# Attention and gated MLP on one core: the first batch in two halves of its queries, its projections woven into the same batch

## The chip, the cores and the metric

The kernel runs on 1 core of one Trainium2 chip. The metric is the device time of one execution in microseconds (us). The engines are PE (TensorE: matmuls and transposes), PEld (its weight loads), ACT (ScalarE), DVE (VectorE), POOL (GpSimd) and SP (SyncE, which here only starts DMAs); PSUM is the memory that the matmuls write.

## The reference, cut to what matters

```
q, k, v: (8 batches, 8 heads, 576 tokens, 64)
scores = q k^T / 8;  keep scores >= rowmax - tau;  softmax of those;  attn = softmax v
x  = attn, as (4608 tokens, 512)
h  = x w_in            (512 -> 2048)
g  = h * clip(h + 3, 0, 6) / 6
out = g w_out          (2048 -> 512)
```

## The kernel before

Two heads make a pair, two pairs a "quad", and a quad is worked off in nine slots: four blocks of 128 queries for each pair, and one slot for the 64 rest queries of both. The program is a loop of 144 slots, 18 to a batch, and a tail. In each slot the engines do this:

```python
for n, sl in enumerate(queue):
    ...
    exp(previous slot) x2                     # ACT
    sm_max(sl)                                # DVE: copy scores out of PSUM, row maximum; POOL: bias = tau - max
    if slot != 8 and todo1:                   # one projection step: 8 matmuls with w_in, relu, gate
        i, j = todo1.pop(0); ...
    sm_recip(prev)                            # DVE: the reciprocal, once per slot
    ... mm2_part(...)                         # quarters of an output tile: 4 matmuls with w_out
    mask(sl) x2                               # ACT
    ... transposes of q and k, or an av product (attn = p v), each evicted from PSUM
    queue[n + 1].tiles = scores(...)          # PE: the next slot's scores
    sm_norm(prev)                             # POOL: normalise x2; SP: DMA transpose of p, for the av product
    start(loads, 2 if n < 3 else 1)           # q and k, by SP
    start(vcasts, 1 if n else 0)              # v, cast to bf16, issued by POOL
    if n > 6:
        start(casts, 1)                       # w_in then w_out, cast to bf16, issued by POOL
```

Each engine works in the program's order here: what stands waits for its own data, and what is behind it waits too. Batch 0's projections are handed over at slot 22, when all its heads and queries are done. The scores take PSUM from a pool of two tiles, av and the q/k transposes share one PSUM tile.

## Time and profile before

| | |
|---|---|
| time | 592.41 us median of 3 |
| span of the profiled execution | 589.8 us |
| busy: PE, ACT, DVE, POOL | 94%, 81%, 70%, 52% |
| first reciprocal, that of slot 18, of slot 63 | 15.56, 72.10, 232.00 us |

The reciprocal occurs once a slot, so its start times are a clock of the slots ("slot n" below is the stretch from the n-th reciprocal to the next). The lines of the profile that carry the argument stand in the prediction. To them I add the first batch in one stretch (stretch, its length, busy us and count on PE, PEld, DVE, ACT, POOL, then granted clock of PE, DMA share, GB/s), and the waits in it (engine and line, what it waited for, total us, times, longest).

```profile
15.56:72.10 56.54, 44.59 (x241) 24.18 (x240) 29.24 (x90) 52.35 (x123) 42.78 (x87) 0.84 1.12 174
```

```profile
ACT s L218 <- POOL bias L213: 3.9, 4, 1.8
```

```profile
PE tp L152 <- ACT qT L156: 4.2, 3, 1.9
PE s L189 <- DVE s L210: 2.3, 3, 0.9
PE av L245 <- ACT kT L174: 2.2, 2, 2.0
```

ACT is busy 52.35 of 56.54 us (the fourth busy figure).

### The profile page before, as it was taken

How to read it: one execution, taken by the hardware profiler on the slowest of the kernel's cores; microseconds unless marked ns; L12 is line 12 of the kernel's file. 1: busy time of each engine (PE TensorE's matmuls, PEld its weight loads, DVE VectorE, ACT ScalarE, POOL GpSimd, SP SyncE). 2: the span in 40 equal slices, each digit the busy share in tenths (PEclk: the TensorE clock that was granted, in tenths of full speed). 3: DMA queues.
4: the chain of work that ended last, by engine and by line, in shares of the span. 5: the costliest groups of instructions: out<-in, count | busy, mean ns of one | idle time of the engine just before them, and what ended most of it. 6: DMA issues, size and time to landing. Idle time of an engine off the chain costs nothing. (4 is left out here: it accounts for less than half of the span.)

```text
span 589.8 us, 11554 instructions
## 1 busy us (share of the span) xinstructions
PE 552.3 (94%) x3840; PEld 319.8 (54%) x3840; DVE 412.4 (70%) x1008; ACT 480.0 (81%) x1078; POOL 305.5 (52%) x646
## 2 busy tenths in 40 slices
PE   6887698889999999999999999999999999999997
PEld 3544354545556555656556565655556565554663
DVE  1545467777878887888868787888868787872350
ACT  4999899798889898898878988898879989881340
POOL 0769676875555555654555555654555555550000
PEclk9978689989999999999999999999999999999999
DMA  5999999999697768976697758985698746552101
GB/s 116 142 178 191 180 152 192 163 177 154 132 154 150 154 119 152 152 155 137 140 137 155 151 119 163 141 162 126 133 138 158 153 101 108 97 110 69 54 19 71
DMA packets 269498, 80.45 MB, mean 136 GB/s; under 512 B 252544, under 2 KB 264832, under 8 KB 269440
## 3 DMA queue, kind: packets, MB, share of 16 engines
q1 hardware_dynamic: 252032, 70.81, 63.4%
q0 software_dynamic: 17408, 8.92, 13.5%
q8 instruction: 30, 0.49, 0.4%
q14 instruction: 28, 0.23, 0.1%
HBM read 36.70 MB, written 9.44 MB: 78 GB/s over the span
## 5 line engine op out<-in xcount | busy, mean ns | idle before, releaser
L230 POOL TENSOR_SCALAR pn<-s,rinv 128x576 bf16<-128x576 f32 x288 | 211.6, 745 | 143.8 <-issue 89.3
L210 DVE TENSOR_SCALAR_CACHE_REDUCE s<-s 128x576 f32<-128x576 f32 x288 | 206.7, 755 | 86.6 <-PE s L189 69.1
L218 ACT ACTIVATE s<-s,bias 128x576 f32<-128x576 f32 x288 | 207.3, 767 | 56.1 <-POOL bias L213 55.3
L222 ACT ACTIVATE s<-s 128x576 f32<-128x576 f32 x288 | 192.9, 672 | 0.4
L189 PE MATMUL s<-kT,qT 64*128 64x288 f32 x1024 | 178.2, 450 | 3.4 <-DVE s L210 2.3
L274 PE MATMUL h<-xT,w_in_sb 128*128 128x288 bf16 x1024 | 144.6, 287 | 3.5 <-DVE g L290 2.8
L302 PE MATMUL o<-w_out_sb,g 128*128 128x512 bf16 x576 | 139.9, 379 | 3.9 <-DVE osb L310 3.9
L274 PEld LDWEIGHTS <-w_in_sb 128*128 128x128 bf16 x1024 | 91.6, 98 | 65.8 <-issue 21.1
L189 PEld LDWEIGHTS s<-kT,qT 64*128 64x128 f32 x1024 | 98.6, 195 | 49.7 <-DVE s L210 12.8
L290 DVE SCALAR_TENSOR_TENSOR g<-r,h 128x576 bf16<-128x576 f32 x128 | 96.5, 754 | 26.1 <-ACT r L282 23.3
L213 POOL TENSOR_SCALAR bias<-m 128x1 f32<-128x1 f32 x288 | 54.6, 190 | 79.0 <-DVE s L210 58.3
L302 PEld LDWEIGHTS <-g 128*128 128x128 bf16 x576 | 55.6, 98 | 59.6 <-issue 9.9
L284 DVE TENSOR_SCALAR r<-h 128x576 f32<-128x576 f32 x81 | 61.0, 753 | 0.0
L222 ACT ACTIVATION_READ_ACCUMULATOR s<-s 128x1 f32 x288 | 54.4, 189 | 0.0
L282 ACT ACTIVATE r<-h,three 128x576 f32<-128x576 f32 x47 | 34.5, 736 | 12.3 <-PE h L274 11.8
L245 PE MATMUL av<-pT,vm 128*64 128x512 bf16 x256 | 36.0, 405 | 8.0 <-ACT kT L174 6.3
L310 DVE TENSOR_SCALAR osb<-o 128x512 f32<-128x512 f32 x30 | 20.3, 678 | 29.3 <-PE o L302 28.6
L245 PEld LDWEIGHTS <-vm 128*64 128x64 bf16 x512 | 20.3, 112 | 33.5 <-issue 26.8
L225 DVE RECIPROCAL rinv<-rsum 128x2 f32<-128x2 f32 x144 | 23.0, 160 | 21.2 <-ACT s L222 20.8
L308 ACT ACTIVATE osb<-o 128x512 f32<-128x512 f32 x6 | 3.6, 597 | 30.4 <-PE o L302 30.4
L152 PE MATMUL tp<-identf,km 128*128 128x128 f32 x128 | 20.9, 288 | 7.1 <-ACT qT L156 7.1
L258 DVE CAST xT<-av 128x512 bf16<-128x512 f32 x32 | 21.8, 682 | 6.3 <-PE av L249 6.3
(32 smaller groups left out, 270.5 us busy)
## 6 DMA issues: line engine op xcount, KB each, us to landing
qm<-in_q_dram SPq DMA_DIRECT2D x64, 128.0 KB, 3.1
km<-in_k_dram SPq DMA_DIRECT2D x64, 128.0 KB, 3.0
out_dram<-osb SPq DMA_DIRECT2D x32, 256.0 KB, 2.6
vm<-in_v_dram POOLq DMA_DIRECT2D x16, 256.0 KB, 5.9
pT<-pn SPq DMA_TRANSPOSE x128, 3.5
w_in_sb<-in_moe_w_in_dram POOLq DMA_DIRECT2D x16, 128.0 KB, 4.1
w_out_sb<-in_moe_w_out_dram POOLq DMA_DIRECT2D x16, 128.0 KB, 3.6
qr<-in_q_dram SPq DMA_DIRECT2D x16, 64.0 KB, 2.7
```

The lines of the kernel that those rows point to most:

```text
L189: nc.tensor.matmul(tiles[a][:, hf, 0:HALF], qkT[pair][0][a * 64:(a + 1) * 64, t * P:(t + 1) * P], keys(pair, a, hf), start=True, stop=True)
L210: nc.vector.tensor_scalar(out=sl.s[:, i, :].rearrange("p (a b) -> p a b", a=2), in0=ps[:, :, 0:HALF], scalar1=1.0, scalar2=None, op0=Alu.m ...
L213: nc.gpsimd.tensor_scalar(out=sl.bias[:, i:i + 1], in0=sl.m[:, i:i + 1], scalar1=-1.0, scalar2=tau, op0=Alu.mult, op1=Alu.add)
L218: nc.scalar.activation(out=s, in_=s, func=Act.Prelu, bias=sl.bias[:, i:i + 1], alpha=REJECT)
L222: nc.scalar.activation(out=s, in_=s, func=Act.Exp, accum_out=sl.rsum[:, i:i + 1])
L230: nc.gpsimd.tensor_scalar(out=pn[:, i, :], in0=sl.s[:, i, :], scalar1=sl.rinv[:, i:i + 1], scalar2=1.0, op0=Alu.mult, op1=Alu.mult)
L245: nc.tensor.matmul(ps[a * 64:(a + 1) * 64, :], vm[:, 2 * hp + a, c * D:(c + 1) * D], pT[:, 5 * a + c, cols], start=(c == 0), stop=False)
L274: nc.tensor.matmul(hps[:, hf, 0:HALF], w_in_sb[:, ki, ni * P:(ni + 1) * P], xT[b][:, ki, hf * HALF:(hf + 1) * HALF], start=(ki == 0), stop ...
L282: nc.scalar.activation(out=r[:], in_=hps[:, :, 0:HALF], func=Act.Relu, bias=three[:])
L284: nc.vector.tensor_scalar(out=r[:], in0=hps[:, :, 0:HALF], scalar1=3.0, scalar2=0.0, op0=Alu.add, op1=Alu.max)
L290: nc.vector.scalar_tensor_tensor(out=g.rearrange("p (a b) -> p a b", a=2), in0=r[:], scalar=6.0, in1=hps[:, :, 0:HALF], op0=Alu.min, op1=A ...
L302: nc.tensor.matmul(o_ps[0], gbuf[:, ni, mt * P:(mt + 1) * P], w_out_sb[:, ni, :], start=(ni == 0), stop=(ni == NI - 1))
```

## The change

The intent: while the first batch runs, PE has nothing to project, and later it is the bound. So batch 0's queries are taken in two halves over all heads. After the first half (256 tokens) its projections can start, eleven slots earlier (the first step in slot 12 instead of 23). This needs q and k of all four pairs early, and the weights early.

```diff
-    qk_pool = ctx.enter_context(tc.tile_pool(name="qk", bufs=4))
+    qk_pool = ctx.enter_context(tc.tile_pool(name="qk", bufs=6))
...
+    for i in range(2):
+        transpose_main(1, i)()          # pair 1, ahead of the first scores
...
+    for half in range(2):
+        for pair in range(NPAIR):
+            for t in (2 * half, 2 * half + 1):
+                slot(pair, t, lambda pair=pair, t=t: first_dst(pair, t))
+            job(8 * half + 2 * pair + 5, lambda pair=pair, half=half: av_main(
+                pair, pts[(pair // 2, half)], (pair % 2) * 256, 256 * half, 256))
+    for quad in range(2):
+        slot(2 * quad, 4, lambda quad=quad: rest_dst(quad))
+        job(20 + quad, lambda quad=quad: av_rest(quad))
+    job(11, lambda: todo1.extend(moe_part(0, 0, 256, (0, 1))))
+    job(21, lambda: todo1.extend(moe_part(0, 256, 320, (2, 3))))
+    job(0, lambda: (alloc_qk(2), alloc_qk(3)) and transpose_main(2, 0))
...
-        if n > 6:
-            start(casts, 1)
+        if n > 2:
+            start(casts, 2)
```

(Cut: the bookkeeping that turns fixed slots into a list of jobs, the projection step with parts of 256 or 320 tokens, and the earlier start of the q and k loads of pairs 2 and 3. From batch 1 on all jobs stand in the same slots as before.)

More of the change, by code (lines that the diff above doesn't have):

```diff
@@ L180, in keys, with scores @@
         return kT[a * 64:(a + 1) * 64, c0:c0 + HALF]
-    def scores(quad, slot):
+    def scores(sl):
         tiles = [ps_s.tile([P, 2, 512], F32, tag="s", name="s") for _ in range(2)]
         for hf in range(2):
-            if slot < 8:
-                pair, t = 2 * quad + slot // 4, slot % 4
+            if sl.t < 4:
+                pair, t = sl.pair, sl.t
                 for a in range(2):
@@ L193, in scores @@
                     for a in range(2):
-                        pair = 2 * quad + n
+                        pair = sl.pair + n
                         nc.tensor.matmul(tiles[a][n * 64:(n + 1) * 64, hf, 0:HALF],
@@ L198, in scores @@
         return tiles
-    class Slot:
-        pass
     def sm_max(sl):
@@ L231, in sm_norm @@
                                     op0=Alu.mult, op1=Alu.mult)
-        if sl.slot < 8:
-            pair, t = 2 * sl.quad + sl.slot // 4, sl.slot % 4
-            dst = pts[pair][:, :, t * P:(t + 1) * P]
-        else:
-            dst = ptr[sl.quad][:, :, :]
+        dst = sl.dst()
         nc.sync.dma_start_transpose(out=dst, in_=pn[:].rearrange("p a b -> p (a b)"))
@@ L249, in av, with av_main @@
             nc.tensor.matmul(ps[r, :], vr[r, hp, :], pT[r, 4, cols], start=False, stop=True)
-    def av_main(pair):
+    def av_main(pair, pT, c0, o0, n):
         b, hp = divmod(pair, NPAIR)
-        if hp == 0:
+        if hp == 0 and b not in xT:
             xT[b] = x_pool.tile([P, KI, S], BF16, tag="xT", name="xT")
         ps = ps_m.tile([P, 512], F32, tag="m", name="av")
-        av(ps[:], pair, pts[pair], slice(0, 512))
-        o0 = 64 if b % 2 else 0
-        nc.vector.tensor_copy(out=xT[b][:, hp, o0:o0 + 512], in_=ps[:])
+        av(ps[:, 0:n], pair, pT, slice(c0, c0 + n))
+        o0 += 64 if b % 2 else 0
+        nc.vector.tensor_copy(out=xT[b][:, hp, o0:o0 + n], in_=ps[:, 0:n])
     def av_rest(quad):
@@ L267, in av_rest, with mm1, mm1_gate @@
                               in_=ps[:, 0:P].rearrange("p (a b) -> p a b", a=2))
-    def mm1(b, ni, pool=None):
+    def mm1(item, pool=None):
+        b, parts, w = item
         hps = (pool or ps_h).tile([P, 2, 512], F32, tag="s" if pool else "h", name="h")
-        for hf in range(2):
+        for n, (ni, c0) in enumerate(parts):
             for ki in range(KI):
-                nc.tensor.matmul(hps[:, hf, 0:HALF], w_in_sb[:, ki, ni * P:(ni + 1) * P],
-                                 xT[b][:, ki, hf * HALF:(hf + 1) * HALF], start=(ki == 0), stop=(ki == KI - 1))
-        return hps
+                nc.tensor.matmul(hps[:, n, 0:w], w_in_sb[:, ki, ni * P:(ni + 1) * P],
+                                 xT[b][:, ki, c0:c0 + w], start=(ki == 0), stop=(ki == KI - 1))
+        return hps[:, :, 0:w]
     def mm1_relu(hps, on_act):
-        r = r_pool.tile([P, 2, HALF], F32, tag="r", name="r")
+        w = hps.shape[2]
+        r = r_pool.tile([P, 2, 320], F32, tag="r", name="r")[:, :, 0:w]
         if on_act:
-            nc.scalar.activation(out=r[:], in_=hps[:, :, 0:HALF], func=Act.Relu, bias=three[:])
+            nc.scalar.activation(out=r, in_=hps, func=Act.Relu, bias=three[:])
         else:
-            nc.vector.tensor_scalar(out=r[:], in0=hps[:, :, 0:HALF], scalar1=3.0, scalar2=0.0, op0=Alu.add,
-                                    op1=Alu.max)
-        return r
-    def mm1_gate(b, ni, hps, r):
-        g = gbuf[:, ni, (b % 2) * S:(b % 2 + 1) * S]
-        nc.vector.scalar_tensor_tensor(out=g.rearrange("p (a b) -> p a b", a=2), in0=r[:], scalar=6.0,
-                                       in1=hps[:, :, 0:HALF], op0=Alu.min, op1=Alu.mult)
+            nc.vector.tensor_scalar(out=r, in0=hps, scalar1=3.0, scalar2=0.0, op0=Alu.add, op1=Alu.max)
+        return r
+    def mm1_gate(item, hps, r):
+        b, parts, w = item
+        o0 = (b % 2) * S
+        (n0, c0), (n1, c1) = parts
+        if n0 == n1:
+            g = gbuf[:, n0, o0:o0 + S].rearrange("p (a b) -> p a b", a=2)
+        else:
+            g = gbuf[:, n0:n0 + 2, o0 + c0:o0 + c0 + w]
+        nc.vector.scalar_tensor_tensor(out=g, in0=r, scalar=6.0, in1=hps, op0=Alu.min, op1=Alu.mult)
     o_ps = {}
@@ L324, in flush, with quarters, moe_part @@
         late.clear()
+    def quarters(bb, mts):
+        return [(bb, mt, part) for mt in mts for part in range(4)]
     def moe_of(b):
-        one = [(b, ni) for ni in range(NI)]
-        two = [(b // 2, mt, part) for mt in (range(4) if b % 2 == 0 else range(4, 9)) for part in range(4)]
-        return one, two
+        one = [((b, ((ni, 0), (ni, HALF)), HALF), ()) for ni in range(NI)]
+        one[-1] = (one[-1][0], quarters(b // 2, range(4) if b % 2 == 0 else range(4, 9)))
+        return one
+    def moe_part(b, c0, w, mts):
+        one = [((b, ((ni, c0), (ni + 1, c0)), w), ()) for ni in range(0, NI, 2)]
+        one[-1] = (one[-1][0], quarters(b // 2, mts))
+        return one
     alloc_qk(0)
@@ L335, with slot, job @@
     transpose_rest((0, 1))()
+    for i in range(2):
+        transpose_main(1, i)()
+    class Slot:
+        pass
     queue = []
-    for quad in range(NQUAD):
-        for slot in range(NSLOT):
-            sl = Slot()
-            sl.quad, sl.slot = quad, slot
-            queue.append(sl)
-    queue[0].tiles = scores(0, 0)
+    jobs = {}
+    def slot(pair, t, dst):
+        sl = Slot()
+        sl.pair, sl.t, sl.dst = pair, t, dst
+        queue.append(sl)
+    def job(n, f):
+        jobs.setdefault(n, []).append(f)
@@ new lines, in new_pT, with rest_dst, first_dst @@
+    def new_pT():
+        return pt_pool.tile([P, 9, 512], BF16, tag="pT", name="pT")
+    def rest_dst(quad):
+        ptr[quad] = ptr_pool.tile([P, 9, P], BF16, tag="pR", name="pR")
+        return ptr[quad][:, :, :]
+    def first_dst(pair, t):
+        key = (pair // 2, t // 2)
+        if pair % 2 == 0 and t % 2 == 0:
+            pts[key] = new_pT()
+        c0 = (pair % 2) * 256 + (t % 2) * P
+        return pts[key][:, :, c0:c0 + P]
+    for half in range(2):
[4 more added lines that the diff above has]
+                pair, pts[(pair // 2, half)], (pair % 2) * 256, 256 * half, 256))
@@ new lines @@
+    for quad in range(2):
[4 more added lines that the diff above has]
+    job(0, lambda: (alloc_qk(2), alloc_qk(3)) and transpose_main(2, 0))
+    job(1, lambda: transpose_main(2, 1))
+    job(2, lambda: transpose_rest((2, 3)))
+    job(3, lambda: transpose_main(3, 0))
+    job(4, lambda: transpose_main(3, 1))
@@ new lines, with main_dst @@
+    job(12, lambda: (alloc_qk(4), alloc_qk(5)) and transpose_main(4, 0))
+    job(14, lambda: transpose_main(4, 1))
+    job(16, lambda: transpose_rest((4, 5)))
+    def main_dst(pair, t):
+        if t == 0:
+            pts[pair] = new_pT()
+        return pts[pair][:, :, t * P:(t + 1) * P]
+    for quad in range(2, NQUAD):
+        p0 = 2 * quad
+        for pair in (p0, p0 + 1):
+            for t in range(4):
+                slot(pair, t, lambda pair=pair, t=t: main_dst(pair, t))
+        slot(p0, 4, lambda quad=quad: rest_dst(quad))
+        n0 = NSLOT * quad
+        job(n0 + 1, lambda p0=p0: transpose_main(p0 + 1, 0))
+        job(n0 + 2, lambda p0=p0: transpose_main(p0 + 1, 1))
+        if quad + 1 < NQUAD:
+            job(n0 + 5, lambda p0=p0: (alloc_qk(p0 + 2), alloc_qk(p0 + 3)) and transpose_main(p0 + 2, 0))
+            job(n0 + 6, lambda p0=p0: transpose_main(p0 + 2, 1))
+            job(n0 + 7, lambda p0=p0: transpose_rest((p0 + 2, p0 + 3)))
+        job(n0 + 8, lambda p0=p0: av_main(p0, pts[p0], 0, 0, 512))
+        job(n0 + 12, lambda p0=p0: av_main(p0 + 1, pts[p0 + 1], 0, 0, 512))
+        job(n0 + 13, lambda quad=quad: av_rest(quad))
+        if quad % 2:
+            job(n0 + 13, lambda quad=quad: todo1.extend(moe_of(quad // 2)))
@@ L345 @@
+    queue[0].tiles = scores(queue[0])
     prev = None
     for n, sl in enumerate(queue):
-        quad, slot = sl.quad, sl.slot
-        b, g = divmod(quad, 2)
-        if slot in (0, 4):
-            pts[2 * quad + slot // 4] = pt_pool.tile([P, 9, 512], BF16, tag="pT", name="pT")
-        if slot == 8:
-            ptr[quad] = ptr_pool.tile([P, 9, P], BF16, tag="pR", name="pR")
-        if quad == 0 and slot == 0:
+        quad, slot_n = divmod(n, NSLOT)
+        if n == 0:
             load_quad(1)
-        if slot == 4 and quad + 2 < NQUAD:
+            start(loads, 5)
+        if slot_n == 4 and quad + 2 < NQUAD:
@@ L356 @@
             load_quad(quad + 2)
-        if slot == 0 and g == 1 and b + 1 < B:
-            load_v(b + 1)
+        if slot_n == 0 and quad % 2 and quad // 2 + 1 < B:
+            load_v(quad // 2 + 1)
         if prev is not None:
@@ L362 @@
         sm_max(sl)
-        if slot != 8 and todo1:
-            i, j = todo1.pop(0)
-            h = mm1(i, j)
-            r = mm1_relu(h, on_act=(slot in (0, 3)))
-            mm1_gate(i, j, h, r)
-            if j == NI - 1:
-                todo2.extend(moe_of(i)[1])
+        if (slot_n != 8 or quad < 2) and todo1:
+            item, then = todo1.pop(0)
+            h = mm1(item)
+            mm1_gate(item, h, mm1_relu(h, on_act=(slot_n in (0, 3))))
+            todo2.extend(then)
         if prev is not None:
@@ L373 @@
         outs = []
-        for _ in range((2, 1, 1, 0, 1, 1, 1, 1, 1)[slot]):
+        for _ in range((2, 1, 1, 0, 1, 1, 1, 1, 1)[slot_n]):
             if todo2:
@@ L381 @@
             sm_mask(sl, i)
-        evict = None
-        nxt = 2 * quad + 2
-        if slot in (1, 2):
-            evict = transpose_main(2 * quad + 1, slot - 1)
-        elif slot == 3 and quad > 0:
-            av_main(2 * quad - 1)
-        elif slot == 4 and quad > 0:
-            av_rest(quad - 1)
-            if quad % 2 == 0:
-                todo1.extend(moe_of(quad // 2 - 1)[0])
-        elif slot in (5, 6, 7) and quad + 1 < NQUAD:
-            if slot == 5:
-                alloc_qk(nxt)
-                alloc_qk(nxt + 1)
-            evict = transpose_main(nxt, slot - 5) if slot < 7 else transpose_rest((nxt, nxt + 1))
-        elif slot == 8:
-            av_main(2 * quad)
-        if evict:
-            evict()
+        for f in jobs.get(n, ()):
+            evict = f()
+            if evict:
+                evict()
         if n + 1 < len(queue):
-            queue[n + 1].tiles = scores(queue[n + 1].quad, queue[n + 1].slot)
+            queue[n + 1].tiles = scores(queue[n + 1])
         if prev is not None:
@@ L406 @@
         late.extend(outs)
-        start(loads, 2 if n < 3 else 1)
+        start(loads, 1)
         start(vcasts, 1 if n else 0)
-        if n > 6:
-            start(casts, 1)
+        if n > 2:
+            start(casts, 2)
         prev = sl
@@ L416, with rest1, rest2, rest @@
     sm_norm(prev)
-    last = NQUAD - 1
-    steps = 0
-    def rest1(i, j):
-        nonlocal steps
-        h = mm1(i, j, pool=ps_s if steps % 3 else None)
-        steps += 1
-        mm1_gate(i, j, h, mm1_relu(h, on_act=True))
-    outs2 = 0
-    def rest2(items):
-        nonlocal outs2
-        for bb, mt, part in items:
-            mm2_part(bb, mt, part, pool=ps_s if outs2 % 3 else None)
+    count = [0, 0]
+    def rest1(item, then):
+        h = mm1(item, pool=ps_s if count[0] % 3 else None)
+        count[0] += 1
+        mm1_gate(item, h, mm1_relu(h, on_act=True))
+        todo2.extend(then)
+    def rest2():
+        while todo2:
+            bb, mt, part = todo2.pop(0)
+            mm2_part(bb, mt, part, pool=ps_s if count[1] % 3 else None)
             if part == 3:
                 flush()
-                late.extend(mm2_out(bb, mt, on_act=(outs2 % 2 == 0)))
-                outs2 += 1
-    while todo1:
-        i, j = todo1.pop(0)
-        rest1(i, j)
-        if j == NI - 1:
-            todo2.extend(moe_of(i)[1])
-    av_main(2 * last + 1)
-    rest2(todo2)
-    av_rest(last)
-    one, two = moe_of(B - 1)
-    for i, j in one:
-        rest1(i, j)
-    rest2(two)
+                late.extend(mm2_out(bb, mt, on_act=(count[1] % 2 == 0)))
+                count[1] += 1
+    def rest():
+        while todo1:
+            rest1(*todo1.pop(0))
+    n0 = NSLOT * NQUAD
+    rest()
+    jobs[n0 + 3][0]()
+    rest2()
+    for f in jobs[n0 + 4]:
+        f()
+    rest()
+    rest2()
     flush()
```

## The prediction

> **What bounds the kernel now.** I read the page first, then the busy time of each engine in stretches, then the times of single instructions. The program is a loop of 144 slots (16 groups of four heads, nine slots each; a batch is 18 slots), then a tail. VectorE does one small reciprocal per slot, so the timeline of these gives the slot clock: the first is at 15.56 us, the one of slot 9 at 41.01, 18 at 72.10, 27 at 102.71, 36 at 135.87, 45 at 167.32, 54 at 199.94; from there a group takes 32.1 to 34.2 us, mostly 32.6. I asked for the busy time between these marks (stretch, its length, busy us and count on PE, PEld, DVE, ACT, POOL, then granted clock, DMA share, GB/s):
>
> ```profile
> 0.00:15.56 15.56, 9.66 (x32) 6.06 (x32) 3.04 (x10) 6.88 (x16) 1.27 (x9) 1.00 0.48 110
> 15.56:41.01 25.45, 21.47 (x102) 11.75 (x100) 13.36 (x42) 24.68 (x59) 18.67 (x38) 0.87 1.07 168
> 41.01:72.10 31.09, 23.12 (x140) 12.43 (x140) 15.88 (x49) 27.67 (x65) 24.11 (x49) 0.83 1.17 180
> 72.10:102.71 30.61, 27.40 (x180) 16.29 (x179) 20.29 (x58) 28.87 (x67) 21.51 (x46) 0.90 1.08 173
> 102.71:135.87 33.16, 27.74 (x204) 16.85 (x203) 24.97 (x63) 28.61 (x67) 24.10 (x49) 0.95 1.11 170
> 135.87:167.32 31.45, 30.23 (x226) 17.68 (x224) 25.67 (x64) 28.83 (x67) 18.21 (x39) 1.00 0.80 138
> 167.32:199.94 32.62, 32.62 (x242) 18.95 (x240) 26.36 (x65) 28.95 (x67) 19.31 (x40) 1.00 0.90 155
> ```
>
> The reader is to see two regimes. From 167 us PE is busy the whole group, so PE sets the time. In the first four groups PE has 3 to 8 us idle per group and a granted clock of 0.83 to 0.95: ACT (97% busy in the first group) and at times POOL set the time. The PE-full group is only 1 to 2 us longer than the groups without projections: there is little to win by taking PE work away.
>
> The second view is the POOL timeline in the second group, where loads of v and casting weight loads are issued by POOL:
>
> ```profile
> 42.88 0.80 POOL L103 DMA_DIRECT2D vm<-in_v_dram  x1
> 43.68 0.54 POOL L117 DMA_DIRECT2D w_in_sb<-in_moe_w_in_dram  x1
> 44.30 0.46 POOL L213 TENSOR_SCALAR bias<-m 128x1 f32<-128x1 f32 x2
> 44.85 1.47 POOL L230 TENSOR_SCALAR pn<-s,rinv 128x576 bf16<-128x576 f32 x2
> 46.26 0.80 POOL L103 DMA_DIRECT2D vm<-in_v_dram  x1
> ```
>
> One slot of POOL here is 46.26 - 42.88 = 3.38 us: bias pair, normalise pair, v issue, one weight issue. The page doesn't count issues as busy, yet POOL does nothing else meanwhile, and the next bias stands behind them. ACT, whose own slot is two exponentials (0.67 each) and two masks (1.34), 2.68 us, then waits:
>
> ```profile
> 44.51 1.44 ACT L218 ACTIVATE s<-s,bias 128x576 f32<-128x576 f32 x2 [1.00 <-POOL bias L213]
> ```
>
> **What the Trainium skill says.** "DMA: Bandwidth & Descriptors", section "SWDGE vs HWDGE vs iDMA": a DMA that casts can only be issued by GpSimd, whose own cores write the descriptors; the trace agrees, with 0.54 to 0.60 us of POOL per weight load and 0.65 to 0.93 per v load. "TensorE: Matmul & The Clock Gate", section "What's actually happening": a PE with idle windows of about 3.4 us falls to half its clock; the 0.83 and 0.87 of the first two groups agree, and 1.00 in the full ones. "Perfetto Trace Analysis", section "Optimization Strategy": where the most contended engine changes over time, interleaving the regimes can help. That is this change's intent.
>
> **The change, part by part.** A projection step is one slot's w_in product (8 matmuls); a quarter is a fourth of an output tile (4 matmuls).
>
> Does the tail shrink? No. I listed the order of the work queue: batch 1 and all later batches are handed over at the same slots as before (batch 1 at slot 40, the last ones at slot 130 and after the loop), one step per slot. What moves is batch 0 alone: its 16 steps from slots 23 to 40 to slots 12 to 19 and 22 to 29, its 16 quarters from slots 40 to 54 to 20 to 36. So 54 slots and the start change, the rest should be as before.
>
> Start. Two more transpose rounds precede the first scores. A round is 6.31 - 4.54 = 1.77 us (PE about 1.1, ACT 0.6). The last eviction before them ends at 9.91; then 1.77 + 1.10 puts the scores at about 12.8 instead of 9.4 (when their second pair of weights was loaded): +3.4. Slot 0 now also has an eviction, 0.5 on ACT. Together **+3.9 us**. (The loads of heads 2 and 3 are issued by 7.5 us and take about 3: in time.)
>
> Slots 1 to 17. POOL without issues is 3.38 - 0.80 - 0.54 = 2.04, say 2.09 with gaps. Weight loads go from one per slot (slots 7 to 38) to two (slots 3 to 18): POOL 2.09 + 2 x 0.58 = 3.25 us, above ACT's 2.68 and above its 3.16 with a 0.48 eviction; with v 3.9 to 4.05. The larger of POOL and ACT by slot: slots 1 and 2 (ACT 3.16, 3.77) 6.9; slots 3 and 4 with v 7.8; slots 5 to 8 13.0; slots 9 to 12 with v 15.9; slots 13 to 17 16.75 (slot 16 has six small evictions, 3.77). Sum 60.4. The same count for before gives 53.4, where 56.5 was measured (72.10 - 15.56): 3.1 us of it are other waits, mainly the av product at slot 8 standing behind the evictions of slot 7 (2.0 us, "PE av L245 <- ACT kT L174" in the waits). With half-sized av products away from the evictions, I keep 1.2 of these: 61.6. That is **+5.1 us**. PE gets 8 matmuls of 256 columns, about 1.0 us a slot (8 x 144.6/1024 = 1.13 for 288), and fits: 2.1 to 2.5 us of other work below POOL's 3.25. DVE adds relu and gate, about 1.3, and comes to some 3.2, just within.
>
> Slots 18 to 62, by group of nine. Removing PE work saves little, as ACT holds a group near 30. A full group's 32.6 has 8 steps (9.0 us) and 9 quarters (9 x 139.9/144 = 8.7), so 14.9 of other PE work.
> - 18 to 26: 7 steps, 8 quarters instead of 4 and none: about 32.0 against 30.6, +1.4.
> - 27 to 35: 3 steps, 8 quarters instead of 8 and none; PE 26, no weight issues any more: about 30.6 against 33.2, -2.6.
> - 36 to 44: 3 steps, 2 quarters instead of 8 and 5: about 30.0 against 31.45, -1.4 (before had no projections in slots 18 to 22 either and was no faster there: 13.6 us, against 13.9 with them in slots 36 to 40).
> - 45 to 53: 8 steps, no quarters instead of 9: about 31.0 against 32.6, -1.6.
> - 54 to 62: 5 quarters instead of 7: -0.5.
>
> Sum **-4.7 us**. In all 3.9 + 5.1 - 4.7 = +4.3: 596.7; I take 596, as the loss at POOL may be partly hidden.
>
> **Rivals.** (a) *The idle PE time is filled and the later groups get all of it.* PE is idle 4.0 + 8.0 + 3.2 + 5.4 us in four groups and slowed by the clock; if the 16 steps and 16 quarters (18.0 + 15.5 us) were free there and their removal paid later, it would be -10 to -20: 575 to 582. Against it: ACT 28.8 to 29.0 us in every group, and 31.09 us in a group with no projections at all. (b) *PE fills, its clock rises.* More PE work may hold the clock at 1.00 and remove the slow scores behind the waits: worth up to 3 to 5 us of the 13% to 17% lost in two groups; 589 to 592. For it: later groups run at 1.00. Against: slots 1 to 11 get no projection. (c) *DMA becomes the limit.* DMA share is already 1.07 to 1.17 and transposes land in 4.8 to 5.5 us there against 3.4 later. Twice the weight loads could lift this to 7 or 8 us; the av products have some 8 us (2.5 slots) after the last transpose they need. If late, PE stops in order: 600 to 606.
>
> **Range and chances.** The start's loss is firm within 1 us, POOL's within 3, the later gain within 3. So 596, 8 in 10 within 588 to 603. Faster by 2% (below 580.6) needs rival (a): 0.03. Slower by 2% (above 604.3) needs (c): 0.06. Within: 0.91.
>
> **What would show it.** First reciprocal at about 19.5; slot 18 at 80 to 82 (before 72.1), with POOL's bias named in ACT's waits of slots 3 to 17 and POOL spacing 3.2 us or more; group 27 to 35 at about 30.6 and 36 to 53 together at 61; from slot 63 the same slot lengths and a tail of the same length (about 62 us from the last reciprocal, 527.5). The prediction is wrong if POOL shows idle time between issues, if slot 18 comes before 77, or if the tail is shorter.

## The result, and the profile after

The changed kernel takes 601.74 us (median of 4, 600.83 to 603.07); the kernel before, in the same rounds, 592.89. A ratio here is the mean time of one kernel's fast runs over that of the other's in the same rounds, so it is not quite the ratio of the medians: 1.0148, with a 95% interval of 1.0118 to 1.0178. So it is slower, by about 9 us or 1.5%, which is less than the 2% that the prediction calls a change.

The slot clock shows where. The last column is how much later the changed kernel is:

| reciprocal | before | after | later by |
|---|---|---|---|
| first | 15.56 | 19.58 | 4.0 |
| of slot 18 | 72.10 | 87.70 | 15.6 |
| of slot 27 | 102.71 | 120.07 | 17.4 |
| of slot 36 | 135.87 | 149.51 | 13.6 |
| of slot 45 | 167.32 | 178.64 | 11.3 |
| of slot 54 | 199.94 | 210.22 | 10.3 |
| of slot 63 | 232.00 | 241.18 | 9.2 |
| of slot 144 | 527.46 | 536.65 | 9.2 |

From slot 63 to the end the two traces run in step: the difference stays at 9.2 us in every group. The busy time in stretches, columns as in the prediction, the first line the first batch (slots 1 to 17), the others the groups of nine slots from 18 to 62:

```profile
19.58:87.70 68.12, 49.58 (x308) 29.53 (x305) 36.73 (x105) 53.20 (x123) 53.14 (x106) 0.82 1.18 167
87.70:120.07 32.37, 30.96 (x236) 17.79 (x239) 24.19 (x62) 28.52 (x67) 17.77 (x38) 1.00 0.79 154
120.07:149.51 29.44, 26.45 (x185) 14.40 (x184) 20.24 (x57) 27.21 (x65) 19.17 (x39) 1.00 1.04 161
149.51:178.64 29.13, 25.25 (x186) 15.30 (x185) 20.89 (x56) 28.68 (x67) 16.89 (x37) 1.00 0.78 158
178.64:210.22 31.58, 27.55 (x204) 16.99 (x203) 24.84 (x63) 28.62 (x67) 19.35 (x40) 0.95 0.84 144
210.22:241.18 30.96, 30.15 (x223) 17.69 (x224) 25.61 (x65) 28.86 (x67) 16.70 (x36) 1.00 0.67 121
```

The first batch took 68.12 us instead of 56.54. ACT's work is the same (53.20 against 52.35) and PE's is 5.0 us more, at 49.58 of 68.12, so neither is full: both stand. In the later groups PE is no longer busy all the time, and the groups end at 29 to 32 us, near what ACT needs. The waits of the first batch:

```profile
PE av L238 <- DMA pT<-pn: 4.7, 2, 2.8
PE av L242 <- DMA vr<-in_v_dram: 3.3, 1, 3.3
PE s L189 <- DVE s L207: 2.4, 3, 0.9
```

```profile
ACT s L215 <- POOL bias L210: 14.8, 13, 3.6
```

There are two new kinds of wait on PE, both for DMAs, and ACT's wait for POOL's bias grew from 3.9 to 14.8 us. The timeline tells how they hang together. It is slot 5, in order of start (start, duration, engine, line, what; in brackets the idle time before it and its releaser):

```profile
31.98 0.66 POOL L107 DMA_DIRECT2D vr<-in_v_dram  x1
32.19 0.89 PE L238 MATMUL av<-pT,vm 128*64 128x256 bf16 x8 [0.39 <-ACT kT L158]
...
36.59 0.42 PE L242 MATMUL av<-pT,vr 64*64 64x256 bf16 x1 [3.29 <-DMA vr<-in_v_dram]
36.94 2.29 PE L189 MATMUL s<-kT,qT 64*128 64x288 f32 x8
...
39.34 0.76 DVE L207 TENSOR_SCALAR_CACHE_REDUCE s<-s 128x576 f32<-128x576 f32 x1 [1.87 <-PE s L189]
...
40.20 0.18 POOL L210 TENSOR_SCALAR bias<-m 128x1 f32<-128x1 f32 x1 [3.30 <-DVE s L207]
40.42 1.45 ACT L215 ACTIVATE s<-s,bias 128x576 f32<-128x576 f32 x2 [3.62 <-POOL bias L210]
```

The second vr load was issued at 31.98 and the av product began at 32.19; PE stood 3.29 us for the load. The next slot's scores stand behind the av product in PE's queue, the maximum behind the scores, the bias behind the maximum, the mask behind the bias. ACT's 3.62 us "for POOL" come down this chain from the one load, so the name at the end of a chain is not its cause. The slot took 7.18 us. In slot 13 the same happens with transposed probabilities:

```profile
67.24 1.07 PE L238 MATMUL av<-pT,vm 128*64 128x256 bf16 x8 [2.85 <-DMA pT<-pn]
```

Behind each of the two waits the granted clock of PE is 0.50 (third figure from the end of each line), and the eight scores matmuls that come next take 2.29 us (from 36.94) and 2.08 us (from 68.59), against 1.24 at a granted 1.00 (from 61.05). So each of the two slots loses about another 1 us. That the wait brought the low clock is not shown; it is 0.50 at other places of the stretch too.

```profile
36.20:46.44 10.24, 8.92 (x35) 4.98 (x35) 3.89 (x12) 5.83 (x13) 6.06 (x14) 0.50 0.98 157
66.92:70.33 3.41, 3.09 (x18) 1.94 (x18) 0.42 (x1) 2.77 (x6) 2.88 (x6) 0.50 1.33 209
```

And this is POOL around slot 11, where it sets the slot's length by itself, 63.64 - 59.58 = 4.06 us from one normalise pair to the next:

```profile
59.58 1.47 POOL L227 TENSOR_SCALAR pn<-s,rinv 128x576 bf16<-128x576 f32 x2
60.99 0.66 POOL L107 DMA_DIRECT2D vr<-in_v_dram  x1
61.65 1.09 POOL L121 DMA_DIRECT2D w_out_sb<-in_moe_w_out_dram  x2
62.82 0.46 POOL L210 TENSOR_SCALAR bias<-m 128x1 f32<-128x1 f32 x2
63.64 1.47 POOL L227 TENSOR_SCALAR pn<-s,rinv 128x576 bf16<-128x576 f32 x2 [0.36 <-DVE rinv L222]
```

### The profile page after: what moved, and what is told of

Its sections match the earlier page's. It is cut to its first block, busy times and chain, and to the rows that moved or that the text cites. A ratio compares the mean times of both kernels' runs of the same rounds, so it can differ in the third digit from the quotient of the medians.

```text
span 599.0 us, 11585 instructions
## 1 busy us (share of the span) xinstructions
PE 547.7 (91%) x3833; PEld 320.3 (53%) x3880; DVE 412.0 (69%) x1012; ACT 479.7 (80%) x1078; POOL 306.6 (51%) x646
## 5 line engine op out<-in xcount | busy, mean ns | idle before, releaser
L189 PE MATMUL s<-kT,qT 64*128 64x288 f32 x1024 | 175.4, 448 | 2.7 <-DVE s L207 2.5
L270 PE MATMUL h<-xT,w_in_sb 128*128 128x288 bf16 (+2 forms) x1024 | 145.0, 287 | 5.5 <-DVE g L292 4.8
L303 PE MATMUL o<-w_out_sb,g 128*128 128x512 bf16 x529 | 132.4, 379 | 6.8 <-DVE osb L311 4.2
L292 DVE SCALAR_TENSOR_TENSOR g<-r,h 128x576 bf16<-128x576 f32 (+2 forms) x128 | 96.5, 754 | 28.3 <-ACT r L279 25.5
L303 PEld LDWEIGHTS <-g 128*128 128x128 bf16 x576 | 55.0, 98 | 62.2 <-issue 12.8
L281 DVE TENSOR_SCALAR r<-h 128x576 f32<-128x576 f32 (+2 forms) x81 | 61.0, 753 | 0.2
L238 PE MATMUL av<-pT,vm 128*64 128x512 bf16 (+1 forms) x288 | 36.5, 377 | 13.4 <-ACT kT L174 6.2
L279 ACT ACTIVATE r<-h,three 128x576 f32<-128x576 f32 (+2 forms) x47 | 34.6, 737 | 11.9 <-PE h L270 11.5
L238 PEld LDWEIGHTS <-vm 128*64 128x64 bf16 x544 | 22.1, 112 | 38.3 <-issue 28.9
L311 DVE TENSOR_SCALAR osb<-o 128x512 f32<-128x512 f32 x30 | 20.3, 677 | 28.9 <-PE o L303 28.6
L251 DVE CAST xT<-av 128x512 bf16<-128x512 f32 (+1 forms) x36 | 22.4, 621 | 10.5 <-PE av L242 10.5
L152 PE MATMUL tp<-identf,qm 128*128 128x128 f32 x128 | 20.6, 287 | 8.5 <-DMA qm<-in_q_dram 4.6
```

Of the source, the lines that this page charges most:

```text
L189: nc.tensor.matmul(tiles[a][:, hf, 0:HALF], qkT[pair][0][a * 64:(a + 1) * 64, t * P:(t + 1) * P], keys(pair, a, hf), start=True, stop=True)
L238: nc.tensor.matmul(ps[a * 64:(a + 1) * 64, :], vm[:, 2 * hp + a, c * D:(c + 1) * D], pT[:, 5 * a + c, cols], start=(c == 0), stop=False)
L270: nc.tensor.matmul(hps[:, n, 0:w], w_in_sb[:, ki, ni * P:(ni + 1) * P], xT[b][:, ki, c0:c0 + w], start=(ki == 0), stop=(ki == KI - 1))
L279: nc.scalar.activation(out=r, in_=hps, func=Act.Relu, bias=three[:])
L281: nc.vector.tensor_scalar(out=r, in0=hps, scalar1=3.0, scalar2=0.0, op0=Alu.add, op1=Alu.max)
L292: nc.vector.scalar_tensor_tensor(out=g, in0=r, scalar=6.0, in1=hps, op0=Alu.min, op1=Alu.mult)
```

## The experiments

Twelve kernels ran, each timed against the kernel before on the same chip. Theory A, formed from the traces: three costs add up, namely the start (4.0 us), POOL's issues, and two single data waits of about 4 us. The rival, B and later C: the DMA engines are crowded, and a wait taken away at one place comes back at another. "Slots 1 to 17" in this table is the time from the first reciprocal to that of slot 18, "slots 18 to 62" from there to that of slot 63; both are of the profiled execution, the total is the median. The profiled execution was the fastest for the change, batch 1's v later, all together, quarter of the bytes and spread, and the slowest for two weight loads, no weaving, loads before the loop, av two slots later and relaxed.

| kernel | first | slots 1 to 17 | slots 18 to 62 | total | ratio |
|---|---|---|---|---|---|
| before | 15.56 | 56.5 | 159.9 | 592.9 | |
| the change | 19.58 | 68.1 | 153.5 | 601.7 | 1.0148 |
| vr first | 19.55 | 69.7 | 153.4 | 601.5 | 1.0170 |
| batch 1's v later | 20.04 | 62.2 | 152.8 | 595.9 | 1.0097 |
| pair 1 later | 16.45 | 75.2 | 153.4 | 604.2 | 1.0217 |
| before, two weight loads | 15.71 | 67.3 | 156.2 | 597.3 | 1.0093 |
| quarter of the bytes | 22.34 | 63.4 | 153.5 | 599.7 | 1.0116 |
| no weaving | 19.94 | 67.4 | 163.1 | 609.5 | 1.0278 |
| loads before the loop | 29.27 | 60.3 | 159.3 | 605.4 | 1.0190 |
| all together | 23.09 | 63.2 | 158.1 | 605.0 | 1.0212 |
| av two slots later | 19.58 | 62.9 | 163.5 | 603.5 | 1.0170 |
| relaxed | 19.87 | 57.7 | 169.4 | 604.1 | 1.0193 |
| relaxed, pair 1 later | 16.73 | 65.3 | 164.0 | 606.9 | 1.0260 |
| spread | 19.49 | 56.8 | 160.4 | 598.8 | 1.0125 |

### vr first

```diff
-        (large v loads, vm)
-        (small v loads, vr)
+        (small v loads, vr)
+        (large v loads, vm)
```

> The changed kernel, but of the four v loads of a batch the two small ones (vr, the rest rows) are issued before the two large ones, so vr is issued two slots earlier. Theory A (the 3.3 us in which PE's first av product stands for vr in slot 5 is one late issue, and costs all of its time): slot 5 falls from 7.2 to about 3.3 us, slot 9's reciprocal comes 3.5 to 4 us earlier (47 instead of 50.6), and the total falls by 3 to 4 us from 601.7. Rival B (the DMA engines are jammed, a wait only moves): slot 5 falls but slots 6 to 13 give it back, total within 1 us of 601.7. The large vm loads now come later and could be waited for instead; if so slot 5 stays above 5 us.

Slot 5 fell from 7.18 to 4.99 us (PE now stood 1.3 us for the large loads, vm), but slot 9 rose from 3.57 to 7.77 and slot 15 from 3.2 to 7.3: av then stood for transposes. Slot 13 fell to 3.6.

```profile
PE av L238 <- DMA pT<-pn: 8.9, 4, 3.8
PE tp L152 <- DMA qm<-in_q_dram: 4.6, 1, 4.6
```

The first line has 8.9 us where the changed kernel has 4.7 (the second is the start's load, as in every run). The total stayed, as B said: the wait moved, though one part of it went further than the slots 6 to 13 that B named.

### Batch 1's v later

```diff
-        if slot_n == 0 and quad % 2 and quad // 2 + 1 < B:
-            load_v(quad // 2 + 1)
+        if (n == 18) if quad < 3 else (slot_n == 0 and quad % 2 and quad // 2 + 1 < B):
+            load_v(1 if n == 18 else quad // 2 + 1)
```

> The changed kernel, but the four v loads of batch 1 are issued in slots 18 to 21 instead of 9 to 12 (they are needed from slot 26). Theory A (in slots 9 to 12 POOL carries two weight issues and a v issue and sets the slot at 3.9 to 4.1 us, and the transposes are late at slot 13 because 2 MB of v are loaded at the same time): slots 9 to 12 fall to about 3.25 us each (-2.5 to -3), slot 13 falls from 7.2 to 3.3 or 4 (-3 to -4), slot 18's reciprocal at 81 to 82 instead of 87.7, total 595 to 597. Rival B (the weight loads alone jam the DMA engines): slot 13 keeps a wait of over 2 us for the transposed probabilities, total 599 to 600.

(A batch's v is 1.2 MB in f32, not the 2 MB that I wrote.) Slot 13 fell from 7.16 to 3.20 us, and no product waited for transposes in the first batch. Slots 9 to 12 did not fall to 3.25 but to 3.6 on average ((64.47 - 49.98) / 4 us). The total is 5.9 us shorter; one of its four runs was at 602.77. Up to slot 8 this kernel is the changed one, yet slot 5 took 5.34 us here and 7.18 there, and slots 1 to 8 29.9 and 31.1: so 1.1 of the 5.9 us between the two profiles in slots 1 to 17 is not the edit, and 4.8 is. Of two edits that remove a wait, this one pays, and it is the one that takes load out of the crowded stretch.

### Pair 1 later

```diff
-    for i in range(2):
-        transpose_main(1, i)()
...
+    job(0, lambda: transpose_main(1, 0))
+    job(1, lambda: transpose_main(1, 1))
```

(The transposes of pairs 2 and 3 each move one or two slots later.)

> The changed kernel, but pair 1 is transposed in slots 0 and 1 as in the kernel before, and pairs 2 and 3 one slot later or in the same slot, so two transpose rounds leave the time before the first scores. Theory A (the start costs 3.4 to 3.9 us that nothing hides): first reciprocal at 16 to 16.5 instead of 19.6, slot 9's reciprocal 2 to 3.5 us earlier (the vr wait in slot 5 may take some of it back), total 598.5 to 600. Rival B (the early slots stand for loads, so an earlier start only waits longer at slot 5): total 601 to 602.

The start was won, 16.45 instead of 19.58, and by slot 5 it was lost: transposes, evictions and scores stood in each other's way in slots 2 to 4 (5.81 us in slot 2). Slots 5 and 13 then stood longer, 7.80 and 8.77 us. The total is 2.4 us worse, outside what either theory gave. So the start's 4 us are not a price that can be refunded alone.

### The kernel before, with two weight loads per slot

```diff
-        if n > 6:
-            start(casts, 1)
+        if n > 2:
+            start(casts, 2)
```

> The kernel before with one edit: weight loads two per slot from slot 3 instead of one per slot from slot 7, nothing else of the change. It tells what the earlier weight loads cost by themselves. Theory A (POOL sets 3.25 us in slots 3 to 18, up to 4.1 with v): slot 18's reciprocal 4 to 7 us later than 72.1, later groups 1 to 2 us shorter as POOL is free there, total 594 to 597. Rival B (POOL's issues are hidden behind ACT and only the new order of queries makes the waits): slot 18 within 1.5 us of 72.1, total 591 to 593.5.

This one edit in the kernel before made slots 1 to 17 take 67.3 us instead of 56.5; the changed kernel has 68.1. It has no new order of queries and no woven projections. Its waits in that stretch are of the changed kernel's kinds, without the one for vr:

```profile
PE av L245 <- DMA pT<-pn: 4.2, 1, 4.2
PE ar L245 <- DMA pR<-pn: 2.5, 1, 2.5
```

```profile
ACT s L218 <- POOL bias L213: 14.3, 12, 4.2
```

Theory A expected slot 18 to be 4 to 7 us later; it was 10.9, in the slowest of the four executions (599.0; median 597.3), so 9 to 11 is the safer reading. Part is won back in slots 18 to 62, where no weights are left to load.

### A quarter of the bytes

The weight tiles are filled with a constant, and each load brings 128 of its 512 columns, so POOL issues as many loads. Its output is wrong, which doesn't matter for the time.

```diff
-                    out=w_in_sb[:, ki, n4 * 512:(n4 + 1) * 512],
+                    out=w_in_sb[:, ki, n4 * 512:n4 * 512 + 128],
...
+    nc.vector.memset(w_in_sb[:], 0.02)      (and w_out_sb)
```

> The changed kernel, wrong on purpose: the weight tiles are filled with a constant at the start and each of the 32 weight loads brings only 128 of its 512 columns. POOL issues as many loads at the same slots, the DMA engines move a quarter of the weight bytes. Theory C (after the first runs: what is lost in slots 3 to 17 is mostly the DMA engines, which carry weights, v, q, k and the transposes at once, so that the transposed probabilities and vr land late): transposes land in under 5 us instead of 6.2, the waits of av for them are gone, slot 18's reciprocal at 78 to 82 instead of 87.7, total 592 to 596. Theory D (POOL's 0.55 us per issue sets the slot): the issues take as long as before, slots 3 to 17 keep 3.2 us or more, slot 18 at 86 or later, total 600 to 602. A mix gives 83 to 86.

The start is 2.8 us later here: the trace shows the two fills on DVE for 6.88 us each, the second until about 17.9, and the first row maximum starts only then instead of at 15.21. So only the time from the first reciprocal is read. Slots 1 to 17 took 63.4 us, 4.7 less than with all the bytes. Transposes landed sooner. Here is the time from issue to landing (minimum, median, maximum) in the first 90 us, for the changed kernel and then for this one:

```profile
DMA to landing us min/median/max: 5.0/6.3/10.0
```

```profile
DMA to landing us min/median/max: 3.7/4.0/7.9
```

What is left is 63.4 - 56.5 = 6.9 us over the kernel before. Slots 5 and 13 still take 5.21 and 4.82 us (3.21 and 2.80 in the kernel before), which is 4.0 of it, and PE still waits 1.7 us for vr and 0.7 for transposes. In the other slots, mostly 3.0 to 3.9 us, ACT's waits for POOL's bias (10.1 us in 14 pieces of at most 1.6 over the stretch) fit POOL's issues, of which there are as many as in the changed kernel. So the result is the mix that I had named: about 5 us of bytes and 7 of the rest, and the rest is not POOL's alone.

### No weaving

```diff
-    job(11, lambda: todo1.extend(moe_part(0, 0, 256, (0, 1))))
-    job(21, lambda: todo1.extend(moe_part(0, 256, 320, (2, 3))))
+    job(22, lambda: todo1.extend(moe_of(0)))
```

> The changed kernel, but batch 0's projections are handed over whole at slot 22, as in the kernel before; the order of queries, the start and the early loads stay. It tells what the weaving itself is worth. My sum says that the steps in slots 12 to 19 cost little (0 to 2 us) and that slots 18 to 62 give back about 6 us, so without it the total should be 4 to 6 us longer than the changed kernel: 605 to 608, slot 18 at 86 to 87.7, slots 27 to 62 as long as in the kernel before (129 us from slot 27 to 63 against 121). Rival: the groups are held by ACT whatever PE does, and the total is within 1.5 us of 601.7.

Slots 1 to 17 kept their length (67.4), so the woven steps cost nothing there. Slots 18 to 62 took 9.6 us more. The weaving is worth about 8 us of the total (609.5 against 601.7, of different rounds; I had said 4 to 6). Not all of this is PE work moved out of full groups: 4.6 of the 9.6 us stand in slots 18 to 26, which took 36.94 us here against 32.37, and there the granted clock is 0.72 where the changed kernel has 1.00 (the second line of its stretches above).

```profile
87.29:124.23 36.94, 31.50 (x198) 18.98 (x194) 20.19 (x56) 29.46 (x67) 18.28 (x41) 0.72 0.83 138
```

### Loads before the loop, and all together

```diff
     nc.vector.memset(three[:], 3.0)
+    start(vcasts, 4)
+    start(casts, 12)
...
-            start(casts, 2)
+            start(casts, 1)
```

> The changed kernel with the loads spread: batch 0's v and the first 12 weight loads are issued before the loop, where POOL is idle from 1.3 to 11.7 us and the DMA share is 0.5, the other 20 one per slot from slot 3. Theory C (the DMA engines are crowded in slots 3 to 17): no wait for vr, shorter waits for transposes, slot 18 at 78 to 82, total 593 to 596; the start may lose up to 2 us as the first q and k loads share the engines. Rival: the start loses what the later slots win, total 599 to 602.

The start lost 9.7 us (in the slowest of four executions, 600.9 to 608.5), and the total, 605.4, is outside what either theory gave. In the first 20 us the q loads, which the first transposes need, took 8.3 us to land in this kernel (first fence) and 2.9 in the changed one (second; the figures are KB and median us to landing):

```profile
qm<-in_q_dram SPq DMA_DIRECT2D x6, 128.0 KB, 8.3
```

```profile
qm<-in_q_dram SPq DMA_DIRECT2D x8, 128.0 KB, 2.9
```

Slots 1 to 17 were then 7.8 us shorter (slot 13 still took 7.3, with batch 1's v where it was), and at slot 23 PE stood 2.96 us for w_out, which now came too late. Adding vr first, batch 1's v later and pair 1 later to it:

> The changed kernel with everything: v and 12 weight loads before the loop with vr first, the other weights one per slot, batch 1's v in slots 18 to 21, pair 1 transposed in slots 0 and 1. If the waits are all removed, slot 18 should come near ACT's and POOL's own time: first reciprocal 16.5, then 17 slots of about 3.2, so 71 to 73, and the later gain of 6 us stays: total 585 to 589, faster than both kernels. If crowded DMA engines only move the wait, as where pair 1 alone was moved: 592 to 597.

It came out at 605.0. My hope of 585 to 589 was far off: the early loads again delayed q and k, and w_out again was waited for at slot 23.

### av two slots later

```diff
-            job(8 * half + 2 * pair + 5, lambda pair=pair, half=half: av_main(
+            job(8 * half + 2 * pair + 7, lambda pair=pair, half=half: av_main(
```

> The changed kernel, but each av product of batch 0 stands two slots later (slots 7, 9, ... 21 instead of 5, 7, ... 19), so that its transposes and vr have two slots more to land; batch 0's first half of projections starts at slot 14 instead of 12. No load is moved or taken away. Theory E (the two stalls of 4 us, in slots 5 and 13, are latency: the product stands too close behind its data): both go, slot 5 at about 3.3 and slot 13 under 4.5 us, slot 18 at 80 to 82, total 594 to 597. Theory C (the DMA engines can't carry the stretch's bytes in the time): the backlog of transposes grows and the stall comes later, in slots 15 to 21; slot 22's reciprocal within 2 us of the changed kernel's 102.5, total 600 to 602.

Both stalls went, slot 5 took 3.32 us and slot 13 4.64, and slot 18's reciprocal came at 82.5, as theory E said. Then slot 20 alone took 10.25 us:

```profile
PE ar L238 <- DMA pR<-pn: 4.1, 1, 4.1
```

The transpose of the rest queries that it stood for took 8.9 us to land (the longest of the stretch, one of slot 8, 11.1), and the later av products met the q/k transposes in the one PSUM tile that they share. All was given back; the median is 1.7 us above the changed kernel's, which is within the scatter (599.2 to 605.7). Neither theory is clean here (slot 22's reciprocal came at 106.3, and theory C had it within 2 us of 102.5): the stalls were indeed products standing too close behind their data, and the backlog did come out later.

### Relaxed, with and without pair 1 later

```diff
+    (av two slots later; batch 1's v in slots 18 to 21; from here as above)
-            start(casts, 2)
+            start(casts, 1)
...
+    job(35, lambda: todo2.extend(quarters(0, range(4))))    # batch 0's w_out quarters from slot 36
```

> The changed kernel with av two slots later as in the run above, one weight load per slot from slot 3 instead of two, batch 1's v in slots 18 to 21, and batch 0's output quarters from slot 36 on (w_out lands by then). So the weaving of the first product and the order of queries stay, and the crowd of loads is gone. Expected: slots 1 to 17 near 57 us (the kernel before has 56.5, with one weight load per slot), slot 18 at 76 to 78, later gain 3 to 5 us as 16 quarters go back to where they were: total 591 to 595. If slots 1 to 17 stay above 61 us, weight loads are not what costs.

Slots 1 to 17 fell to 57.7 us, as expected. Slots 19 to 21 then took 8.86, 6.92 and 5.63: one wait of 3.4 us for the last w_in load, and the same meeting of av products with transposes. The total missed my range by 9 us; its four executions lie between 598.7 and 606.7, and the profiled one is the slowest.

> The run above with pair 1 transposed in slots 0 and 1 instead of ahead of the first scores. With the data waits gone the earlier start should now be kept: first reciprocal at 16.5, slot 18 at 73 to 75, total 3 us under the run above: 588 to 592, at or below the kernel before. If an earlier start is again given back (as it was when pair 1 alone was moved), the total stays within 1 us of the run above.

Again the earlier start was given back, with 7.6 us more in slots 1 to 17, and the median is 2.9 us worse, with ranges that overlap.

### Spread

```diff
-    job(11, lambda: todo1.extend(moe_part(0, 0, 256, (0, 1))))
-    job(21, lambda: todo1.extend(moe_part(0, 256, 320, (2, 3))))
+    job(15, lambda: todo1.extend(moe_part(0, 0, 256, ())))
+    job(21, lambda: todo1.extend(moe_part(0, 256, 320, ())))
+    job(35, lambda: todo2.extend(quarters(0, range(4))))
...  (vr between the two large v loads; batch 1's v in slots 18 to 21)
-            start(casts, 2)
+            start(casts, 1)
```

> Last run: the changed kernel with its loads spread but its av products where the change has them (moving them late made them meet the rest transposes at slots 19 to 21): batch 1's v in slots 18 to 21, vr between the two large v loads, one weight load per slot from slot 3, batch 0's first half of projections from slot 16 (w_in has landed by then), its output quarters from slot 36. Expected if the crowd of loads is the cause of what slots 1 to 17 lose: no wait for vr or transposes over 1.5 us before slot 18, slot 18 at 76 to 79 instead of 87.7 (the start keeps its 4 us), slot 22 at 91 to 94 instead of 102.5, total 589 to 594, level with the kernel before. If slot 18 is later than 82 the crowd is not the cause; if slots 19 to 36 give the gain back, total 597 or more.

Slots 1 to 17 took 56.8 us, the 56.5 of the kernel before, though order and transposes are the changed kernel's. ACT's wait for POOL in them is 4.6 us, where it was 14.8:

```profile
ACT s L215 <- POOL bias L210: 4.6, 6, 2.8
```

One wait of 2.5 us for transposed probabilities is left, in slot 7 (5.7 us), where I had expected none over 1.5:

```profile
PE av L238 <- DMA pT<-pn: 2.8, 2, 2.5
```

But slots 18 to 62 took 160.4 us, no less than in the kernel before (159.9), where the change had 153.5: the later gain is gone. I put this down to the projections and quarters being later; no run moved these alone. The total is 598.8, outside my 589 to 594 (its profiled execution was its fastest, 596.2).

## Why the prediction was right or wrong

The total, 601.7, lies in the stated range of 588 to 603, near its upper end, 5.7 us above the 596 that I named. The mechanism was right in its parts, and one term of the sum was mis-sized: by 6.5 us, twice the "within 3" that I gave it. The range held partly by luck, as the later gain was 1.7 us larger than I said and covered some of it. My sign for slot 18, 80 to 82, failed (87.7). The total also lies in the 600 to 606 of rival (c), and it is (c)'s wait that came.

- **The start, +3.9 us.** Measured: 4.0. Right, though the runs that moved pair 1 back show that it could not be had back alone.
- **Slots 1 to 17, +5.1 us.** Measured: +11.6. This is the step that failed. The count of POOL's and ACT's time gave 60.4 us, to which I added 1.2 for other waits; the trace has 68.1. Two slots, 5 and 13, took 7.2 us each where 3.25 stood in the count; these 7.8 us are more than the whole gap of 6.5. The other fifteen slots took 53.8 us, where the count has 53.9. There POOL was as full as I said: from slot 3 to 15 it was idle 0.25 to 0.41 us a slot, but for 1.2 in slot 7, 3.9 in slot 5 and 3.4 in slot 13. So my sign of being wrong, POOL idle between issues, came true in just the two slots that broke the count. In both PE stood for a DMA. I had this as rival (c) and held it back because an av product stood "some 8 us" behind its last transpose. In the trace the transposes landed in 6.3 us at the median and 10.0 at worst. The worst is the one of slot 13: issued at 57.15, landed at 67.1, while PE was ready for it at 64.4, so the slack was 7.2 us and the landing took 10. For the small vr load I had no line at all: its last part is issued in slot 4 and needed in slot 5.
- **Two misreadings.** I wrote that the page doesn't count POOL's issues as busy. It does: the 42.78 us (x87) of the first batch before are 34 biases, 34 normalises and 19 issues, and the 53.14 (x106) after have 38 issues. POOL's own time for issues rose from 12.2 to 22.8 us. The sum didn't suffer, as it took the issues from the timeline. And "ACT 28.8 to 29.0 us in every group" holds only from slot 18 on (28.6 to 29.0); the two groups before have 24.7 and 27.7.
- **What causes the 11.6 us.** Two runs point at the loads from both sides. Two weight loads per slot put into the kernel before add 10.8 us to the same slots (its slowest profile); one per slot, with batch 1's v moved away, takes 11.3 off the changed kernel in its fastest profile (one vr load comes a slot earlier there and its projections start four slots later too, but taking them out of these slots whole, with the loads left, won less than 1). So the loads are the cause within the 1 to 2 us by which profiles differ, and the new order and the weaving cost little there. How much of it is POOL's issue time and how much the bytes on the DMA engines is less sharp: with a quarter of the weight bytes and all the issues, 4.7 us went. Of the remaining 6.9, 4.0 stand in slots 5 and 13; the rest fits POOL's issues, which no run took away alone. How the two share it stays open.
- **Slots 18 to 62, -4.7 us.** Measured: 159.9 to 153.5, -6.4. By group (+1.4, -2.6, -1.4, -1.6, -0.5 said; +1.8, -3.7, -2.3, -1.0, -1.1 measured) the signs are all right. The PE work taken away came back only in part, as ACT holds a group at about 29: rival (a), 575 to 582, was rightly set aside.
- **The tail.** From the last reciprocal to the end it takes 62.3 us in both, as said.
- **Rival (b), the clock.** In the first batch it did not rise: 0.82, and 0.84 before. In slots 18 to 35 it did, from 0.90 and 0.95 to 1.00, and without the weaving it was 0.72 in slots 18 to 26; so some of the later gain may be the clock, which no run separates from the work moved. The prediction also says that the trace agrees with what it cites from the Trainium skill, "TensorE: Matmul & The Clock Gate", section "What's actually happening": half the clock after idle windows of about 3.4 us. The trace agrees on the half: in the kernel before the granted clock is 0.50 from 30.56 to 37.39, 47.63 to 51.04 and 64.69 to 78.35, which lowers the means. It doesn't show the idling: PE's longest wait in the first batch is 2.0 us.

## What to carry to other kernels

Pulling work earlier pulls its loads earlier too: count what the stretch then asks of the issuing engine and of the DMA engines, before counting the gain on the engine that is to be filled. Where data are waited for in an in-order queue, compare the slack with the landing time in the crowded stretch, not with the average, and remember that the last load in a list of four lands last. A single late load can appear in the waits as another engine's delay several steps further on; follow the chain back to the DMA before choosing an experiment. None of the twelve kernels beat the kernel before; the nearest form of the change, with batch 1's v moved out of the crowd, is 1.0097 of it.

## What the Trainium skill lacked or had wrong

- "DMA: Bandwidth & Descriptors", section "Anatomy of one DMA — SWDGE (gpsimd) path", gives about 2.0 us plus bytes over 436 GB/s for one such DMA. For a weight load of 256 KB read that would be 2.6 us, my estimate from that page. For the loads of w_in the runs show 4.1 us to landing at the median in the kernel before, 5.2 in the changed one and 8.8 for four of them from 52 to 70 us. What is lacking is a figure for how the time grows when several queues share the engines.
- The pages give a bandwidth for a DMA transpose, but none its time from issue to landing. Here it is 3.4 us at the median from 200 to 500 us, and 6.3, at worst 10.0, in the crowded first 90 us of the same kernel; SP's own time for one issue grew with it, from 1.30 to as much as 3.27 us.
- "DMA: Bandwidth & Descriptors", section "Issuing engines are not separate DMA queues", calls the sequencer's time to start a DMA usually small relative to the DMA. The runs agree for one load: on POOL it was 0.54 to 0.66 us for each weight or small v load, and a w_in load landed in 5.2. What is lacking is that these times add up on an engine that also computes: three of them took 1.75 us of a slot of 4.06 (0.66 + 1.09, from 60.99 on), and the bias that ACT needs stood behind them.
